# A three-stage kernel: second block's decays made in the pre-phase, silu issued ahead of the next weight tile's scaling, and block 1's units in steps 0, 1, 3 and 5

## The chip, the cores and the metric

The kernel runs on one core of a Trainium2 chip. The time is device time in microseconds (us) of one launch, as the median of several runs; lower is better. The engines are TensorE (PE, with its weight loads as PEld), VectorE (DVE), ScalarE (ACT), GpSimd (POOL) and the queues of SyncE (SP), each of which works through its own instructions in the order in which they were written.

## The reference

Three computations follow one another. The first is a chunked linear recurrence over 4 batches x 8 heads x 768 tokens (head 32, state 16):

```python
cum = np.cumsum(log(a)); L = np.exp(cum_i - cum_j) * causal      # per chunk of 32
y  = (C B^T * L) @ x + (C @ state) * np.exp(cum)
state = exp(sum) * state + sum_j B_j x_j exp(cum_end - cum_j)
```

The result, laid out as 3072 tokens x 256, goes through a gated layer, and that through a routed layer in which each token takes the one expert of eight with the largest logit:

```python
g = x @ w_gate; x = (g / (1 + exp(-g)) * (x @ w_val)) @ w_out     # 1536 hidden
h = np.maximum(x[mask] @ w1[e], 0); out[mask] = gate_w * (h @ w2[e])   # e = argmax
```

## The kernel before

Tokens are taken as 24 units of 128 tokens (six to a batch) and 6 blocks of 512 tokens (four units each). Block b is ready for the gated layer when its four units have written the tile `xt` of block b.

A unit u is made by these helpers: `weigh` (L268) multiplies x by a decay weight into `xw`, on DVE in the first blocks; `scores_mm` (L276) makes on PE the products of C and B and the sums for the state (both in `pc`); `scores_m` (L296) masks `pc` into `mt` on DVE; `states` (L303) carries the state with two DVE operations (`sv`, `se`) and two ACT copies (`st`); `values_mm` (L326) multiplies on PE into `py`; `values_out` (L352) multiplies by the decays `U` in four DVE operations (`y`, `z`) and casts to the high half of `xt` on ACT; `values_low` (L371) makes the low half on DVE. The decays of a whole block are made by `emit_d` (L247: four ACT operations into the tile `du` for blocks 1 and 2) and `emit_u` (L259: two PE matmuls into `pu`, two ACT copies into `U`).

The gated layer has 12 hidden tiles f of 128. Each number is held as a high and a low half, so each product is three matmuls. The weights arrive as 64-bit numbers (`load_w`) and are decoded for one hidden tile by `decode` (L391) in four parts: part 0 scales the high words into `ha` on ACT; part 1 puts the words together in three DVE operations into `wv`; part 2 casts the high half `wh` on ACT; part 3 makes the low half `wl` on DVE. A step for a block and a hidden tile is `mlp1_mm` (L420: six matmuls into `pg`, six into `pv`, in the order high, high, low of the weights for each half of the contraction), `mlp1_h` (L436: silu of `pg` on ACT into `h`, then times `pv` on DVE), `mlp1_split` (L442: `hh` on ACT, `hl` on DVE) and, two steps later (LAG = 2), `mlp1_down` (L449: six matmuls).

`first_block` writes all this out by hand for blocks 0 and 1. In a pre-phase it makes the four units of block 0, one after another, with matmuls that have no result (`keep_busy`) in PE's gaps. A loop of 24 steps follows: steps 0 to 5 are hidden tiles 0 to 5 of block 0, steps 6 to 11 the same for block 1, steps 12 to 23 the other six tiles of both. The table `units` says which step carries which unit (unit 4 to 7 are block 1, unit 8 and after block 2), the table `todo` which step decodes which hidden tile. Nothing reorders: the order of the code is the order of each engine's queue. PSUM is shared out as three buffers of tag "a" (`pc` and half of `py`, and `pu`), three of tag "g" (`pg`, `pv`, half of `py`), and two for the sums of `mlp1_down`; a matmul that takes a buffer waits until its last reader is done. The SBUF tag "mt" has two buffers, which `mt` and `du` share.

Of the kernel before, what the change touches and what calls it, by code (L numbers as in the profile page):

```python
# [9 lines left out]
F32 = mybir.dt.float32  # L10
# [18 lines left out]
BLK = 512  # L29
# [91 lines left out]
def kernel(  # L121
# [14 lines left out]
    def ps_a(shape, name):  # L136
        return ps.tile(shape, F32, tag="a", bufs=3, name=name)

    def ps_g(name, shape=(128, BLK)):
        return ps.tile(list(shape), F32, tag="g", bufs=3, name=name)  # L140
# [17 lines left out]
    u_t = {}  # L158
# [39 lines left out]
    def keep_busy(n):  # L198

        if not idle_t:  # L200
            idle_t.append(ps.tile([128, 2, 256], F32, tag="y0", bufs=1, name="pi"))
        for _ in range(n):
            nc.tensor.matmul(out=idle_t[0], lhsT=r32[:, 0],  # L203
                             rhs=r32.rearrange("p g j -> p (g j)").unsqueeze(1).to_broadcast([128, 2, 256]),
                             start=True, stop=True)
# [41 lines left out]
    def emit_d(b):  # L247
        d = ap_.tile([128, 4, 128], F32R, name="du", tag="mt", bufs=2)
        o = C_MU + 4 * (b % 2)
        if b in (1, 2):  # L250
            for q in range(4):
                nc.scalar.activation(out=d[:, q], in_=er[:, b // 2, 0:128], func=AF.Copy, scale=c1[:, o + q:o + q + 1])
        else:
            nc.gpsimd.tensor_tensor(
                out=d, in0=er[:, b // 2, 0:128].unsqueeze(1).to_broadcast([128, 4, 128]),
                in1=c1[:, o:o + 4].unsqueeze(2).to_broadcast([128, 4, 128]), op=ALU.mult)
        return d

    def emit_u(b, d=None):  # L259
        if d is None:  # L260
            d = emit_d(b)
        u_t[b] = ap_.tile([128, 4, 4, 64], F32, name="U", tag="U", bufs=1)
        for g in range(2):
            p = ps_a([128, BLK], "pu") if b else ps_g("pu")
            nc.tensor.matmul(out=p, lhsT=r32[:, g], rhs=d.rearrange("p a b -> p (a b)"), start=True, stop=True)
            nc.scalar.copy(out=u_t[b][:, :, 2 * g:2 * g + 2], in_=p.rearrange("p (o a i) -> p o a i", o=4, a=2))

    def weigh(u, e):  # L268

        r = raw[u]  # L270
        b, o = divmod(u, 4)
        r["xw"] = ap_.tile([128, 8, 32], F32, name="xw", tag="xw", bufs=3)
        e.tensor_tensor(out=r["xw"], in0=r["x"], in1=W[:, b, o * 8:o * 8 + 8].unsqueeze(2).to_broadcast([128, 8, 32]),
                        op=ALU.mult)
# [116 lines left out]
    def decode(f, *parts):  # L391


        if f >= NF:
            return
        for part in parts:
            lo, hi = wr[f][:, :, 0], wr[f][:, :, 1]
            if part == 0:
                ha_t[f] = mp.tile([128, 768], F32, name="ha", tag="ha", bufs=2)
                nc.scalar.activation(out=ha_t[f], in_=hi.bitcast(F32), func=AF.Copy, scale=2.0 ** -112)  # L400
            elif part == 1:
                v = wv_t[f] = mp.tile([128, 768], I32, name="wv", tag="wv", bufs=2)
                nc.vector.tensor_scalar(out=v, in0=lo, scalar1=29, scalar2=None, op0=ALU.logical_shift_right)
                nc.vector.scalar_tensor_tensor(out=v, in0=ha_t.pop(f).bitcast(I32), scalar=3, in1=v,
                                               op0=ALU.logical_shift_left, op1=ALU.bitwise_or)
                nc.vector.scalar_tensor_tensor(out=v, in0=hi, scalar=-0x80000000, in1=v,
                                               op0=ALU.bitwise_and, op1=ALU.bitwise_or)
            elif part == 2:
                nc.scalar.copy(out=wh[:, f], in_=wv_t[f].bitcast(F32))
            else:  # L410
                nc.vector.tensor_tensor(out=wl[:, f], in0=wv_t.pop(f).bitcast(F32), in1=wh[:, f].bitcast(F32),
                                        op=ALU.subtract)
# [7 lines left out]
    def mlp1_mm(b, c, m, f):  # L420

        xt = xt_t[b]
        cs = slice(c, c + m)
        p = []
        for i in range(2):
            t = ps_g("pg" if i == 0 else "pv")[:, 0:m]
            n = 0
            for k in range(2):
                o = i * 256 + k * 128
                for w, xp in ((wh, 0), (wh, 1), (wl, 0)):  # L430
                    nc.tensor.matmul(out=t, lhsT=w[:, f, o:o + 128], rhs=xt[:, xp, k, cs], start=n == 0, stop=n == 5)  # L431
                    n += 1
            p.append(t)
        return p
# [355 lines left out]
    def first_block():  # L790

        setup_loads()
        load(0)
        load_w(0)
        load(1)
        load(2)
        load_w(1)
        load(3)
        load_w(2)
        nc.sync.dma_start(out=c2, in_=I["cst"][:, C1:C_END])  # L800
        load_w(3)
        setup_ln()
        setup_ones()
        setup_decay()
        setup_cum(0, 1)
        keep_busy(2)
        weigh(0, nc.vector)
        scores_mm(0)
        cum_split(0, 1)
        scores_m(0)  # L810
        emit_u(0, emit_d(0))
        cum_store(0, 1, cum_ends(0, 1, cum_ends_d(0, 1)))
        states(0)
        cum_pairs(1, 8)
        keep_busy(3)
        decode(0, 0)
        for u in range(4):
            weigh(u + 1, nc.vector)
            scores_mm(u + 1)
            values_mm(u)  # L820
            if u == 1:
                setup_cum(1, 2)
            keep_busy((5, 7, 8, 10)[u])
            decode(u // 2, 3 if u % 2 else 1)
            scores_m(u + 1)
            if u % 2 == 0:
                decode(u // 2, 2)
            values_out(u)
            states(u + 1)
            values_low(u)  # L830
            if u % 2:
                decode(u // 2 + 1, 0)
            load(u + 4)
            if u == 1:
                silu_first()
        d = emit_d(1)
        load_w(4)

        todo = {0: 2, 1: 3, 2: 4, 3: 5, 6: 6, 8: 7, 10: 8, 12: 9, 14: 10, 15: 11}
        units = {0: 4, 1: 5, 3: 6, 4: 7, 13: 8, 16: 9, 19: 10, 22: 11}  # L840
        for i in range(2 * NF):
            q, f = divmod(i, HALF)
            b, f = q % 2, f + HALF * (q // 2)
            u = units.get(i)
            w = todo.get(i, NF)
            if i + 1 in units and units[i + 1] > 4:
                weigh(units[i + 1] + 1, nc.vector if i < 16 else nc.gpsimd)
            if i == 0:
                weigh(5, nc.vector)
            p = mlp1_mm(b, 0, BLK, f)  # L850
            if i == 0:
                emit_u(1, d)
            if u is not None:
                scores_mm(u + 1)
                values_mm(u)
            if len(late) == LAG:
                mlp1_down(*late.pop(0))
            late.append((b, 0, BLK, f))
            decode(w, 1)
            if w < NF:  # L860
                load_w(w + 3)
                decode(w + 1, 0)
            h = mlp1_h(p, BLK)
            decode(w, 2)
            if u is not None:
                values_out(u)
            decode(w, 3)
            if i >= 20:
                turn_y(0, i - 20)
            mlp1_split(h, b, 0, BLK, f)  # L870
            if i in (7, 13):
                take_part(0 if i == 7 else 1)
            if i == 19:
                take_y(0)
            if u is not None:
                values_low(u)
                if u != 7:
                    scores_m(u + 1)
                    states(u + 1)
                load(u + 4)  # L880
            if i == 6:
                scores_m(8)
                cum_split(1, 2)
            if i == 7:
                dd.append(cum_ends_d(1, 2))
            if i == 8:
                cum_store(1, 2, cum_ends(1, 2, dd.pop()))
                cum_pairs(8, NU)
                states(8)
            if i == 9:  # L890
                dd.append(emit_d(2))
            if i == 10:
                emit_u(2, dd.pop())
            if 16 <= i < 20:
                setup_route(i - 16)
            if i == 21:
                dd.append(emit_d(3))
            if i == 23:
                emit_u(3, dd.pop())
# [193 lines left out]
```

## Time and profile before

| | |
|---|---|
| median of 3 runs | 551.43 us (550.49 to 553.5) |
| the profiled execution's own time | 551.91 us |
| its span, first to last instruction | 550.1 us |
| mean granted TensorE clock | 0.981 |
| PE busy | 514.1 us (93%) |
| DVE busy | 298.1 us (54%) |
| ACT busy | 212.8 us (39%) |
| POOL busy | 98.6 us (18%) |

The profiled execution is 0.48 us longer than the median, and its span 1.8 us shorter than its own time. A share of busy time is an average over the whole span; the two blocks that the change touches lie in its first 67 us. Matmuls are pipelined, so that PE's busy time is not PE at its peak.

### The profile page before, as it was taken

Reading aid. Unit: us, or ns where it says so; the run is one execution under the profiler, and the core shown is the slowest. Engines: PE = TensorE matmul, PEld = TensorE weight load, DVE = VectorE, ACT = ScalarE, POOL = GpSimd, SP = SyncE. Lnnn points to the kernel's source line nnn. Section 1 sums busy time; section 2 is a strip of 40 time slices with the busy share of each in tenths; the row PEclk is TensorE's granted clock in tenths of the full one; section 3 lists DMA queues with packets and bytes.
Section 4 is the critical chain, followed back from the end, with each engine's and each line's share of the span. In section 5 each row is a group of like instructions: output and inputs, shape, how many; then the busy total and the mean of one; then the engine's idle time right before and its main releaser. Section 6 shows DMA issues by size and latency. Waiting matters only on the chain.

```text
span 550.1 us, 11255 instructions
## 1 busy us (share of the span) xinstructions
PE 514.1 (93%) x4599; PEld 423.9 (77%) x4599; DVE 298.1 (54%) x648; ACT 212.8 (39%) x394; POOL 98.6 (18%) x120
## 2 busy tenths in 40 slices
PE   5788799999998999999999999999997999999990
PEld 3566688778876777887778778888896999898980
DVE  4879787775453454445443554354374655646320
ACT  3554446533232333333333333434452443544320
POOL 0000000221003040002200034302027424250211
PEclk9899999999999899999999999999998999999995
DMA  8654332121020132103100102434056534431100
GB/s 317 251 174 155 135 108 84 40 50 39 21 98 2 20 98 41 39 20 98 21 1 2 41 2 86 147 116 39 2 192 78 184 94 150 149 113 47 38 11 31
DMA packets 20551, 45.85 MB, mean 83 GB/s; under 512 B 4624, under 2 KB 8080, under 8 KB 20496
## 3 DMA queue, kind: packets, MB, share of 16 engines
q1 hardware_dynamic: 17280, 38.39, 22.3%
q0 software_dynamic: 3072, 6.41, 4.6%
q8 instruction: 37, 0.61, 0.6%
q10 hardware_dynamic: 144, 0.30, 0.2%
q14 instruction: 18, 0.15, 0.1%
HBM read 38.59 MB, written 6.50 MB: 82 GB/s over the span
## 4 chain that ended last, share of the span: by engine, by line
PE 76%; issue 11%; DVE 4%; POOL 2%; ACT 2%; DMA 1%; another core or an unknown queue 1%; SPq 0%; POOLq 0%; ACTq 0%; DVEq 0%
PE py L459 18%; PE pg L431 18%; PE pv L431 17%; PE ph L741 6%; PE po L762 6%; PE pt L543 2%; PE pc L292 2%; POOL out L776 2%; PE pi L203 1%; PE py L348 1%; PE py L338 1%; PE pc L286 1%; PE px L730 1%; POOL xg L700 1%
## 5 line engine op out<-in xcount | busy, mean ns | idle before, releaser
L431 PE MATMUL pg<-xt,wh 128*128 128x512 f32 x288 | 93.7, 407 | 0.9 <-ACT h L438 0.9
L431 PE MATMUL pv<-xt,wh 128*128 128x512 f32 x288 | 90.8, 396 | 1.5 <-DVE h L439 1.5
L439 DVE TENSOR_TENSOR h<-h,pv 128x512 f32<-128x512 f32 x72 | 49.4, 687 | 69.1 <-PE pv L431 57.6
L446 DVE TENSOR_TENSOR hl<-h,hh 128x512 fp32r<-128x512 f32 x72 | 50.1, 695 | 64.1 <-ACT hh L445 61.7
L741 PE MATMUL ph<-xt,hl 128*128 128x512 f32 x288 | 74.0, 399 | 0.0
L762 PE MATMUL po<-hl,hh 128*128 128x256 f32 x384 | 71.3, 286 | 2.8 <-issue 2.8
L431 PEld LDWEIGHTS pv<-xt,wh 128*128 128x128 f32 x288 | 54.4, 189 | 14.7 <-DVE h L439 1.9
L762 PEld LDWEIGHTS po<-hl,hh 128*128 128x128 f32 x384 | 60.8, 190 | 5.2 <-issue 3.2
L431 PEld LDWEIGHTS pg<-xt,wh 128*128 128x128 f32 x288 | 52.6, 190 | 11.8 <-ACT h L438 1.5
L741 PEld LDWEIGHTS ph<-xt,hl 128*128 128x128 f32 x288 | 52.4, 191 | 9.7
L445 ACT CAST hh<-h 128x512 fp32r<-128x512 f32 x72 | 44.6, 620 | 38.8 <-DVE h L439 38.8
L459 PE MATMUL py<-hh,wh 128*128 128x512 f32 x144 | 58.7, 408 | 0.0
L438 ACT ACTIVATE h<-pg 128x512 f32<-128x512 f32 x72 | 42.8, 594 | 39.8 <-PE pg L431 39.6
L431 PE MATMUL pg<-xt,wl 128*128 128x512 f32 x144 | 57.3, 398 | 0.0
L459 PE MATMUL py<-hh,wl 128*128 128x512 f32 x144 | 56.8, 395 | 0.0
L459 PE MATMUL py<-hl,wh 128*128 128x512 f32 x144 | 56.8, 395 | 0.0
L431 PE MATMUL pv<-xt,wl 128*128 128x512 f32 x144 | 56.8, 394 | 0.0
L601 POOL DMA_INDIRECT slots<-ids,si x24 | 25.4, 1058 | 171.0 <-DVE si L593 166.2
L762 PE MATMUL po<-hl,hl 128*128 128x256 f32 x192 | 54.4, 283 | 0.4 <-issue 0.2
L750 DVE SCALAR_TENSOR_TENSOR hl<-ph,hh 128x512 fp32r<-128x512 f32 x48 | 33.1, 689 | 34.3 <-ACT hh L749 32.4
L749 ACT ACTIVATE hh<-ph 128x512 fp32r<-128x512 f32 x48 | 28.8, 600 | 42.0 <-PE ph L741 22.2
L762 PEld LDWEIGHTS po<-hl,hl 128*128 128x128 f32 x192 | 36.5, 190 | 0.9 <-issue 0.4
(140 smaller groups left out, 675.8 us busy)
## 6 DMA issues: line engine op xcount, KB each, us to landing
eraw<-in_ew SPq DMA_DIRECT2D x24, 512.0 KB
wraw<-in_mw SPq DMA_DIRECT2D x12, 768.0 KB
xbb<-in_xbb SPq DMA_DIRECT2D x24, 256.0 KB
cbd<-in_cbd SPq DMA_DIRECT2D x24, 256.0 KB
yd<-yr SPq DMA_DIRECT2D x6, 528.0 KB
slots<-ids,si POOLq DMA_INDIRECT x24
xg<-yd,idx POOLq DMA_INDIRECT x24
out<-ob,idx POOLq DMA_INDIRECT x24
```

The source lines that it names most:

```text
L292: nc.tensor.matmul(out=r["pc"][g][32 * q:32 * q + 32, 0:256], lhsT=r["bt"][k, 32 * q:32 * q + 32], rhs=r["c"][k, q // 2].rearrange("p h i ...
L431: nc.tensor.matmul(out=t, lhsT=w[:, f, o:o + 128], rhs=xt[:, xp, k, cs], start=n == 0, stop=n == 5)
L438: nc.scalar.activation(out=h, in_=p[0], func=AF.Silu)
L439: nc.vector.tensor_tensor(out=h, in0=h, in1=p[1], op=ALU.mult)
L445: nc.scalar.copy(out=hh, in_=h)
L446: e.tensor_tensor(out=hl, in0=h, in1=hh.bitcast(F32), op=ALU.subtract)
L459: nc.tensor.matmul(out=yb[b][d][:, c:c + m], lhsT=w[:, f, o:o + 128], rhs=h, start=first and n == 0, stop=last and n == 2, skip_group_chec ...
L601: i = nc.gpsimd.indirect_dma_start(out=slots[0:E * upto], out_offset=bass.IndirectOffsetOnAxis(ap=si[:, s:s + 1], axis=0), in_=ids[g][:, o ...
L741: nc.tensor.matmul(out=p, lhsT=self.hl[:, w, o:o + 128], rhs=self.xt[:, xp, k], start=n == 0, stop=n == 5)
L749: nc.scalar.activation(out=hh, in_=p, func=AF.Relu)
L750: nc.vector.scalar_tensor_tensor(out=hl, in0=p, scalar=0.0, in1=hh.bitcast(F32), op0=ALU.max, op1=ALU.subtract)
L762: nc.tensor.matmul(out=self.po[s // 2][:, s % 2], lhsT=h[:, q], rhs=self.hl[:, w, o:o + DM], start=f == 0 and n == 0 and s % 2 == 0, stop= ...
```

## The change

Four edits, all in the order in which `first_block` writes its work, and one in a buffer count:

- `emit_d(1)` moves from behind the pre-phase into its second unit (u = 1), and `emit_u(1)` from step 0 of the loop into the pre-phase's third unit (u = 2), where two of the eight matmuls without result are taken out. Its two `pu` tiles are now of tag "g". The tile `U` gets two buffers instead of one.
- In every step `mlp1_h` is written ahead of `load_w` and of part 0 of the next tile's decode.
- Unit 7 moves from step 4 to step 5, and stands there ahead of the step's `mlp1_mm` (its low half, `values_low`, too).
- The decode of hidden tile 5 moves from step 3 to step 4.

```diff
     def emit_u(b, d=None):
...
-        u_t[b] = ap_.tile([128, 4, 4, 64], F32, name="U", tag="U", bufs=1)
+        u_t[b] = ap_.tile([128, 4, 4, 64], F32, name="U", tag="U", bufs=2)
         for g in range(2):
-            p = ps_a([128, BLK], "pu") if b else ps_g("pu")
+            p = ps_a([128, BLK], "pu") if b > 1 else ps_g("pu")
...
             if u == 1:
                 setup_cum(1, 2)
-            keep_busy((5, 7, 8, 10)[u])
+            if u == 1:
+                d = emit_d(1)
+            if u == 2:
+                emit_u(1, d)
+            keep_busy((5, 7, 6, 10)[u])
...
-        d = emit_d(1)
         load_w(4)
 
-        todo = {0: 2, 1: 3, 2: 4, 3: 5, 6: 6, 8: 7, 10: 8, 12: 9, 14: 10, 15: 11}
-        units = {0: 4, 1: 5, 3: 6, 4: 7, 13: 8, 16: 9, 19: 10, 22: 11}
+        todo = {0: 2, 1: 3, 2: 4, 4: 5, 6: 6, 8: 7, 10: 8, 12: 9, 14: 10, 15: 11}
+        units = {0: 4, 1: 5, 3: 6, 5: 7, 13: 8, 16: 9, 19: 10, 22: 11}
...
+            if u == 7:
+                scores_mm(u + 1)
+                values_mm(u)
+                values_out(u)
+                values_low(u)
             p = mlp1_mm(b, 0, BLK, f)
-            if i == 0:
-                emit_u(1, d)
-            if u is not None:
+            if u is not None and u != 7:
                 scores_mm(u + 1)
                 values_mm(u)
...
             decode(w, 1)
+            h = mlp1_h(p, BLK)
             if w < NF:
                 load_w(w + 3)
                 decode(w + 1, 0)
-            h = mlp1_h(p, BLK)
             decode(w, 2)
-            if u is not None:
+            if u is not None and u != 7:
                 values_out(u)
...
             if u is not None:
-                values_low(u)
                 if u != 7:
+                    values_low(u)
                     scores_m(u + 1)
                     states(u + 1)
                 load(u + 4)
```

On ACT, this is what stands before in the pre-phase from the exponential `er` (made in unit 1, the input of `emit_d`) to the cast `wh` of hidden tile 1 in unit 2:

```order
L194 ACTIVATE er<-pe 128x264
L369 CAST xt<-y_329 128x2x128
L321 ACTIVATE st<-se,eb 128x64
L322 ACTIVATE st<-sv,eb 128x64
L400 ACTIVATE ha<-wraw 128x768
L210 ACT_TABLE_LOAD
L210 ACTIVATE sf<-c_69 128x1
L409 CAST wh<-wv 128x768
```

And this is what stands there now:

```order
L194 ACTIVATE er<-pe 128x264
L252 ACTIVATE du<-er,c_69 128x128 x4
L369 CAST xt<-y_334 128x2x128
L321 ACTIVATE st<-se,eb 128x64
L322 ACTIVATE st<-sv,eb 128x64
L400 ACTIVATE ha<-wraw 128x768
L210 ACT_TABLE_LOAD
L210 ACTIVATE sf<-c_69 128x1
L266 COPY U<-pu 128x4x128 x2
L409 CAST wh<-wv 128x768
```

The four `du` operations now stand ahead of unit 1's cast to `xt`, and the two copies to `U` ahead of the cast `wh`.

On ACT at the start of the loop, from the last operations of the pre-phase to the first cast of step 0, before:

```order
L322 ACTIVATE st<-sv,eb 128x64
L400 ACTIVATE ha<-wraw 128x768
L252 ACTIVATE du<-er,c_69 128x128 x4
L266 COPY U<-pu 128x4x128 x2
L400 ACTIVATE ha<-wraw 128x768
L438 ACTIVATE h<-pg 128x512
L409 CAST wh<-wv 128x768
```

And now:

```order
L322 ACTIVATE st<-sv,eb 128x64
L400 ACTIVATE ha<-wraw 128x768
L438 ACTIVATE h<-pg 128x512
L400 ACTIVATE ha<-wraw 128x768
L409 CAST wh<-wv 128x768
```

The first silu (`h`) has nothing of the decays ahead of it, and stands ahead of the scaling `ha` of hidden tile 3.

On DVE, from the low half `hl` of step 2 on, before (the `xw` is unit 8's, the three `wv` are hidden tile 5's, the `h` step 3's, `y` and `z` unit 6's):

```order
L446 TENSOR_TENSOR hl<-h,hh 128x512
L273 TENSOR_TENSOR xw<-xbb,W 128x256
L403 TENSOR_SCALAR wv<-wraw 128x768
L404 SCALAR_TENSOR_TENSOR wv<-ha,wv 128x768
L406 SCALAR_TENSOR_TENSOR wv<-wraw,wv 128x768
L439 TENSOR_TENSOR h<-h,pv 128x512
L364 TENSOR_TENSOR y_869<-py,U 128x192
L365 TENSOR_TENSOR z_870<-py,U 128x64
L366 TENSOR_TENSOR y_869<-py,U 128x64
L367 TENSOR_TENSOR y_869<-y_869,z_870 128x64
L411 TENSOR_TENSOR wl<-wv,wh 128x768
L446 TENSOR_TENSOR hl<-h,hh 128x512
```

Now `h` of step 3 and unit 6's first three operations on `py` follow the `hl` of step 2 at once; then come these (the first `hl` is step 3's, the `mt`, `sv` and `se` are unit 7's, the last `h` is step 4's):

```order
L367 TENSOR_TENSOR y_856<-y_856,z_857 128x64
L446 TENSOR_TENSOR hl<-h,hh 128x512
L375 TENSOR_TENSOR xt<-y_856,xt 128x2x128
L300 TENSOR_TENSOR mt<-pc,c_69 128x256 x2
L316 SCALAR_TENSOR_TENSOR sv<-se,eb,pc 128x64
L319 SCALAR_TENSOR_TENSOR se<-sv,eb,pc 128x64
L273 TENSOR_TENSOR xw<-xbb,W 128x256
L403 TENSOR_SCALAR wv<-wraw 128x768
L404 SCALAR_TENSOR_TENSOR wv<-ha,wv 128x768
L406 SCALAR_TENSOR_TENSOR wv<-wraw,wv 128x768
L439 TENSOR_TENSOR h<-h,pv 128x512
L411 TENSOR_TENSOR wl<-wv,wh 128x768
```

`xw` of unit 8 and the decode of hidden tile 5 now stand behind all of step 3's work and unit 7's state, and unit 7's own `y` follows only after this `wl`.

## Rows read from the trace of the kernel before

**Rows 1.** The page: busy us of the engines, and granted clock in 40 slices.
```profile
PE 514.1 (93%) x4599; PEld 423.9 (77%) x4599; DVE 298.1 (54%) x648; ACT 212.8 (39%) x394; POOL 98.6 (18%) x120
...
PEclk9899999999999899999999999999998999999995
```

**Rows 2.** Waits of PE, 0 to 64 us: who waited <- for whom, us, times, longest.
```profile
PE pc L286 <- DVE sv L316: 1.7, 1, 1.7
PE pv L431 <- DVE h L439: 1.5, 1, 1.5
```

**Rows 3.** Timeline, pre-phase: start us, us, engine, line, operation [idle before <- releaser].
```profile
19.67 0.39 ACT L194 ACTIVATE er<-pe 128x264 f32<-128x264 f32 x1 [3.69 <-PE pe L192]
19.96 0.40 ACT L369 CAST xt<-y 128x256 fp32r<-128x256 f32 x1
...
20.39 0.43 DVE L375 TENSOR_TENSOR xt<-y,xt 128x256 fp32r<-128x256 f32 x1 [0.46 <-ACT xt L369]
...
23.71 0.84 ACT L409 CAST wh<-wv 128x768 fp32r<-128x768 f32 x1 [0.55 <-DVE wv L406]
...
25.17 0.40 ACT L369 CAST xt<-y 128x256 fp32r<-128x256 f32 x1 [0.62 <-DVE y L367]
```

**Rows 4.** Timeline, loop step 0.
```profile
30.42 0.62 PE L431 MATMUL pg<-xt,wh 128*128 128x512 f32 x2
...
30.65 1.27 ACT L252 ACTIVATE du<-er,c 128x128 fp32r<-128x128 f32 x4
...
33.63 1.07 ACT L266 COPY U<-pu 128x512 f32<-128x512 f32 x2 [1.71 <-PE pu L265]
...
35.43 0.61 ACT L438 ACTIVATE h<-pg 128x512 f32<-128x512 f32 x1
...
36.68 0.35 DVE L364 TENSOR_TENSOR y<-py,U 128x192 f32<-128x192 f32 x1
```

**Rows 5.** Timeline, DVE and ACT in loop steps 2 to 4.
```profile
51.98 0.69 DVE L446 TENSOR_TENSOR hl<-h,hh 128x512 fp32r<-128x512 f32 x1
...
52.58 0.42 DVE L273 TENSOR_TENSOR xw<-xbb,W 128x256 f32<-128x256 f32 x1
...
54.49 0.96 DVE L406 SCALAR_TENSOR_TENSOR wv<-wraw,wv 128x768 int32<-128x768 int32 x1
...
55.37 0.68 DVE L439 TENSOR_TENSOR h<-h,pv 128x512 f32<-128x512 f32 x1
55.49 0.83 ACT L409 CAST wh<-wv 128x768 fp32r<-128x768 f32 x1 [2.59 <-DVE wv L406]
...
56.63 0.95 DVE L411 TENSOR_TENSOR wl<-wv,wh 128x768 fp32r<-128x768 f32 x1
...
57.71 0.69 DVE L446 TENSOR_TENSOR hl<-h,hh 128x512 fp32r<-128x512 f32 x1
...
59.62 0.28 DVE L319 SCALAR_TENSOR_TENSOR se<-sv,eb,pc 128x64 f32<-128x64 f32 x1
```

**Rows 6.** Timeline of PE: step 5, start of step 6, and unit 8.
```profile
62.53 0.62 PE L431 MATMUL pg<-xt,wh 128*128 128x512 f32 x2
...
66.71 0.64 PE L431 MATMUL pg<-xt,wh 128*128 128x512 f32 x2
...
99.42 0.34 PE L286 MATMUL pc<-xw,xbb 64*32 64x64 f32 x16
...
100.82 0.50 PE L459 MATMUL py<-hh,wh 128*128 128x512 f32 x1
```

**Rows 7.** The chain that ended last: start us, us, what.
```profile
13.96 2.44 issue
...
174.34 5.28 another core or an unknown queue
...
180.87 2.56 PE pg L431 x6
183.43 1.67 PE pv L431 x6
```

## The prediction

> **What bounds the kernel now.** I read the page first: PE is busy 514.1 us of 550.1, and its granted clock is down in three places only, near 16 us, near 180 us and at the end [rows 1]. So nearly all the time is matmuls that the change doesn't touch, and what it can win are the holes in PE. The waits of PE in the first 64 us came next. Two of them lie in the step of unit 7: 1.7 us until DVE has made `sv`, which frees the buffers for unit 8's products, and 1.5 us until DVE has multiplied `h` [rows 2]. Both times DVE is what is late. Then I read the timelines of the pre-phase and of steps 0 to 4 [rows 3 to 5]. In step 0 the silu `h` begins at 35.43, though PE began the step at 30.42 and needs half of it for `pg`: `du` and the copies to `U`, which wait for PE's `pu`, stand ahead of it on ACT [rows 4]. DVE can only then multiply `h` and go on to unit 4's `y` at 36.68. From there to the last `se` of unit 7 at 59.62 it has almost no idle time, and the steps run at its pace.
>
> From 62.53 PE no longer waits: step 5 takes from 62.53 to 66.71, 4.18 us for its 18 matmuls, or 0.232 us each [rows 6]. Whatever moves the start of step 6, now 66.71, moves the end of the kernel by as much.
>
> **The pre-phase, +1.2 us.** `emit_d(1)` puts four operations ahead of unit 1's cast to `xt`. They took 1.27 us together [rows 4], of which the last overlaps with what comes behind it; I take 1.2 us. Their input `er` is made at 19.67 and the cast followed at 19.96 [rows 3], so the cast now comes at about 21.15. DVE waited for that cast with the low half at 20.39 [rows 3], and behind the low half stands the `xw` of unit 3, on which PE's next products wait. So units 2 and 3 and the loop start later by the 1.2 us: 31.6 instead of 30.42. A second wait is new: `mt` of unit 2 must now wait until PE has read that of unit 1, since `du` has the other buffer. On PE that reading stands ahead of the matmuls for `er`, so it is over before 19.67; `y` follows `mt` within the time that ACT spends on `du`, and I cost it at nothing.
>
> The two copies to `U` (1.07 us [rows 4]) now stand between the silu table's first use and `wh` of tile 1. There ACT was idle for 0.55 us ahead of `wh` and for 0.62 us ahead of the next cast to `xt` [rows 3], 1.17 us together, so they are hidden, with 0.1 us to spare. If that cover fails they cost up to 1.07 us more, which gives 2.3 us as the upper end; the lower end is nothing, if the casts were not what unit 3 waits for. Two matmuls for `pu` take the place of two without result.
>
> **Step 0, -1.9 us.** The two `pu` matmuls go, and `h` has only `ha` of tile 2 ahead of it, which belongs to the pre-phase. PE makes 12 matmuls from 31.6 to 34.4 (2.8 us at 0.232). Unit 4's matmuls follow; an undisturbed unit takes 1.40 us, from 99.42 to 100.82 [rows 6], so `y` of unit 4 can begin on DVE at about 35.9 to 36.0. The silu is done by then, since `pg` is complete at about 33.2. Before, `y` began at 36.68, which is 6.26 us after the loop's start; now it is 4.4 us after it. With the pre-phase DVE is 0.7 us ahead of before.
>
> **Steps 0 to 2, nothing.** DVE has the same operations in the same order from this `y` to the `hl` of step 2, so the 0.7 us stay: that `hl` moves from 51.98 [rows 5] to 51.3. Silu ahead of `ha` buys nothing here, because DVE, not ACT, sets the pace; where ACT has room the order of two of its operations is free. From step 6 on PE doesn't wait in the trace, so there it buys nothing either.
>
> **Steps 3 to 5, -1.1 us.** Now I add up DVE's new row from intervals of the old one [rows 5]. From `hl` to the next operation are 0.6 us: `h` of step 3 at 51.9. From `h` to `hl` of the same step, with unit 6's `y`, its cast on ACT and `hh` between them, 2.34 us (55.37 to 57.71; the `wl` that stood there lay in the wait for `hh`): 54.25. From `hl` over the low half of `xt` and `mt` to `se` 1.91 us: 56.15. Then 0.3 us to `xw` of unit 8, and from `xw` to the last `wv` 1.91 us (52.58 to 54.49): 58.35. From there to `wh` on ACT 1.00 us, and `wh` itself takes 0.83: 60.2. `wl` takes 0.95 us: 61.15.
>
> PE meanwhile has steps 3 and 4 behind it without a wait (`pv` of step 4 needs `h` of step 3, done at 52.6) and stands at unit 8's products at about 56.4. It gets `xw` at 56.9, and is done with unit 7 at 58.3. Now the new wait: step 5 multiplies by hidden tile 5, whose decode was put one step later. PE waits 1.9 us for `wh` until 60.2, does two matmuls, and waits again for `wl` until 61.2. Of the 18 matmuls, ten of the first twelve and the six of `mlp1_down` are left after that, 16 x 0.232 = 3.7 us. Step 6 begins at 64.9 instead of 66.71. So of the 3.2 us of waits that go [rows 2] a good part comes back, as 2.4 us of other waits. The tail of unit 7 isn't late: behind `wl` come `hl`, `y`, a cast and the low half of `xt`, about 2.3 us, done by 63.5.
>
> **The sum.** 1.2 - 1.9 - 1.1 = -1.8 us, so the profiled execution's 551.91 would be 550.1. That execution is 0.48 us over the median; against the median of 551.43 the forecast is 549.6. The second `U` buffer changes nothing that PE waits for later.
>
> **Rivals.** *The clock falls.* The new wait of PE in step 5 is 1.9 us and, two matmuls later, 0.5 us, after another 0.5 us shortly before. In the trace the clock went to half (1.2 of 2.4 GHz) after PE had stood idle for 2.44 us from 13.96 on, and again after the stall at 174.34 [rows 7]; after the single waits of 1.5 and 1.7 us [rows 2] it did not. What stands against it is that the new idle time is broken by two matmuls. The price: after 180.87 six `pg` matmuls took 2.56 us and six `pv` 1.67 us [rows 7] instead of 1.40 each, so 1.4 us more; with what was hit ahead of them I take 1.7. Then the gain is gone: 551.3.
>
> The Trainium skill, TensorE: Matmul & The Clock Gate, Part 1, says that half rate is the default which activity lifts, and that what the gate watches runs freely, not from the kernel's start, so that the point of a change moves between runs. By that rule it is a matter of where the new wait falls, and the time is either 549.6 or 551.3; the trace, in which 2.44 us of idle time were enough, doesn't contradict it.
>
> *PE sets the pace of step 5.* If DVE's row were 2.9 us shorter than I add it up, step 5 would begin at 58.3 and the gain would be 4.7 us: 546.7. For it speaks that DVE's share is only 54% [rows 1]; against it, that every interval in the row was measured under the same load.
>
> *DVE's row is longer: slower.* Four operations in the new row wait for ACT within steps 3 to 5 (`hl`, `wl`, `hl`, the low half of `xt`), and I allowed in full for the first two alone. Step 6 needs the low half of unit 7, which I have at 63.5. Each wait can cost about one cast and its turn, up to 1.2 us. The kernel is slower once unit 7 or `wl` is 1.8 to 3.2 us later than I have it; with four such waits in full, 4.8 us on the last of them, step 6 begins at 68.3, 1.6 us later than before: 553.0. Against it: all of these queues had the same neighbours before.
>
> *The stall at 174.34.* DVE stood 5.28 us there for something the profile doesn't name [rows 7]. The order of instructions there isn't changed. Should another layout make it go, the time would be about 545.
>
> **How the numbers follow.** The forecast gets 0.50, the fallen clock 0.27, PE's pace 0.09, the longer row 0.09, the stall 0.05. The forecast's own range is 548.4 to 550.7, from the bounds of the pre-phase (0 to 2.3 us instead of 1.2). The range that takes in the fallen clock and most of the other cases is 547.0 to 552.3. About 0.5% (2.8 us) is what a measurement of this kernel can tell from no change, so faster means under 548.7 and slower over 554.2. Faster is PE's pace, the stall and a tail of the forecast: 0.24. Slower is a tail of the longer row: 0.04. The rest, 0.72, is no change that can be told.
>
> **What would show it.** In the changed kernel's profile, unit 1's cast to `xt` should begin near 21.2, step 0 near 31.6, `y` of unit 4 near 36.0, and `wl` of tile 5 should end near 61.2 with PE waiting for it and for `wh`; step 6 should begin near 64.9. A step 5 without a wait, a clock at 0.5 between 58 and 66 us, or `U` copies ahead of a late `wh` in the pre-phase would each prove one step wrong.

## The result and the profile after

The changed kernel takes 547.35 us (median of 13 runs, 544.38 to 552.03), the kernel before 551.43 us beside it (13 runs, 547.15 to 554.1). The ratio is 0.9917, with an interval of 0.989 to 0.9943: 0.8% faster, where the forecast was 549.6 us and no change that can be told. The profiled execution went from 551.91 to 547.26 us, its span from 550.1 to 545.5 us.

The page of the changed kernel, the two lines that answer to [rows 1]:

```profile
PE 512.3 (94%) x4597; PEld 422.2 (77%) x4597; DVE 297.8 (55%) x648; ACT 212.7 (39%) x394; POOL 97.5 (18%) x120
...
PEclk9899899999999999999999999999998999999996
```

In the clock row, slice 5 (54.5 to 68 us) has become an 8, and slice 14 (near 180 us), an 8 before, is a 9. Both kernels have a further 8 near 420 us, which the prediction's count of three places left out. So the clock fell at a new place and no longer falls at an old one. The waits of PE up to 66 us (who waited <- for whom: us, times, longest) show what [rows 2] became:

```profile
...
PE pg L431 <- ACT wh L409: 1.8, 1, 1.8
PE py L338 <- DVE h L439: 0.7, 1, 0.7
PE pc L286 <- DVE xw L273: 0.5, 1, 0.5
PE pc L286 <- DVE mt L300: 0.4, 1, 0.4
...
```

The waits for `sv` and for `h` are gone, and the forecast wait of step 5 for `wh` is there with 1.8 us. Next the timeline of the pre-phase and of step 0 (start us, us, engine, line, operation), as [rows 3, 4] before:

```profile
19.79 0.39 ACT L194 ACTIVATE er<-pe 128x264 f32<-128x264 f32 x1 [3.73 <-PE pe L192]
20.08 1.27 ACT L252 ACTIVATE du<-er,c 128x128 fp32r<-128x128 f32 x4
21.25 0.39 ACT L369 CAST xt<-y 128x256 fp32r<-128x256 f32 x1
...
24.46 1.07 ACT L266 COPY U<-pu 128x512 f32<-128x512 f32 x2
25.42 0.85 ACT L409 CAST wh<-wv 128x768 fp32r<-128x768 f32 x1
26.45 0.40 ACT L369 CAST xt<-y 128x256 fp32r<-128x256 f32 x1 [0.19 <-DVE y L367]
...
31.55 0.62 PE L431 MATMUL pg<-xt,wh 128*128 128x512 f32 x2
33.14 0.60 ACT L438 ACTIVATE h<-pg 128x512 f32<-128x512 f32 x1 [1.26 <-PE pg L431]
35.92 0.36 DVE L364 TENSOR_TENSOR y<-py,U 128x192 f32<-128x192 f32 x1 [0.62 <-PE py L348]
```

The loop begins 1.13 us later and unit 4's `y` 0.76 us earlier. (Where step 0 begins differs by up to 1 us between profiles of kernels with the same pre-phase; see below the table.) Then the end of DVE's row and step 5, as [rows 5, 6] before:

```profile
51.23 0.69 DVE L446 TENSOR_TENSOR hl<-h,hh 128x512 fp32r<-128x512 f32 x1
...
56.08 0.28 DVE L319 SCALAR_TENSOR_TENSOR se<-sv,eb,pc 128x64 f32<-128x64 f32 x1
...
59.21 0.83 ACT L409 CAST wh<-wv 128x768 fp32r<-128x768 f32 x1 [1.35 <-DVE wv L406]
60.08 0.96 DVE L411 TENSOR_TENSOR wl<-wv,wh 128x768 fp32r<-128x768 f32 x1 [0.30 <-ACT wh L409]
60.10 0.95 PE L431 MATMUL pg<-xt,wh 128*128 128x512 f32 x2 [1.84 <-ACT wh L409]
61.09 0.80 PE L431 MATMUL pg<-xt,wl 128*128 128x512 f32 x1
...
66.17 0.63 PE L431 MATMUL pg<-xt,wh 128*128 128x512 f32 x2
```

`wl` ends at 61.04, and step 6 begins at 66.17, only 0.54 us earlier than before. Why it isn't earlier is in two stretches of PE (us, busy us and instructions of PE, PEld, DVE, ACT and POOL, granted clock, DMA):

```profile
60.44:63.86 3.42, 3.38 (x9) 2.19 (x8) 2.42 (x7) 1.13 (x3) 0.00 (x0) 0.50 0.83 327
66.20:69.60 3.40, 3.40 (x16) 2.79 (x15) 3.12 (x5) 1.58 (x4) 0.00 (x0) 1.00 0.00 0
```

Nine matmuls ran in 3.42 us at the granted clock of 0.50, where 16 run at 1.00: the clock was at its lower level, 1.2 of 2.4 GHz.

The rest of the gain came where the change had moved nothing. From step 6 to step 28 both kernels keep the same pace, the changed one 0.54 us ahead (step 28 starts at 170.49 and 169.95). Step 29 begins 3.40 us earlier, step 30 4.96 us, and from step 31 on it is about 4.5 us to the end. (Steps 24 to 35 are the hidden tiles of block 2, so step 28 is its fifth, which carries unit 13.) In step 28 PE makes the products `py` of unit 13, and DVE's `y` waits for them. First the rows of the kernel before:

```profile
174.74 0.52 PE L348 MATMUL py<-cbd,st 64*32 64x64 f32 x28
...
179.60 0.36 DVE L364 TENSOR_TENSOR y<-py,U 128x192 f32<-128x192 f32 x1 [5.26 <-remote]
...
180.01 0.85 PE L543 MATMUL pt<-iw,yT 128*128 128x136 f32 x4 [3.17 <-DVE y L364]
```

And the same rows after the change:

```profile
174.18 0.52 PE L348 MATMUL py<-cbd,st 64*32 64x64 f32 x28
...
176.22 0.36 DVE L364 TENSOR_TENSOR y<-py,U 128x192 f32<-128x192 f32 x1 [2.43 <-PE py L348]
...
176.63 0.73 PE L543 MATMUL pt<-iw,yT 128*128 128x136 f32 x4 [0.33 <-issue]
```

In both PE has written `py` long before `y` starts: 4.3 us before, 1.5 us after. That is the 5.28 us row of the chain in [rows 7]. PE stood still for 3.2 us in one and 0.3 us in the other, and only in the kernel before did the clock go to half behind it.

### The profile page after: what moved, and what is told of

The parts are those of the page before. It is cut to its first block, busy times and chain, and to the rows that moved or that the text cites. A ratio compares the mean times of both kernels' runs of the same rounds, so it can differ in the third digit from the quotient of the medians.

```text
span 545.5 us, 11245 instructions
## 1 busy us (share of the span) xinstructions
PE 512.3 (94%) x4597; PEld 422.2 (77%) x4597; DVE 297.8 (55%) x648; ACT 212.7 (39%) x394; POOL 97.5 (18%) x120
## 4 chain that ended last, share of the span: by engine, by line
PE 76%; issue 11%; DVE 5%; POOL 2%; ACT 2%; DMA 1%; another core or an unknown queue 0%; SPq 0%; POOLq 0%; ACTq 0%
PE py L459 18%; PE pg L431 18%; PE pv L431 17%; PE ph L741 7%; PE po L762 6%; PE pt L543 2%; PE pc L292 2%; POOL out L776 2%; PE py L348 1%; PE py L338 1%; PE pi L203 1%; PE pc L286 1%; PE px L730 1%; DVE hl L446 1%; DMA at<-in_at 1%
## 5 line engine op out<-in xcount | busy, mean ns | idle before, releaser
L762 PEld LDWEIGHTS po<-hl,hh 128*128 128x128 f32 x384 | 60.5, 190 | 5.8 <-ACT hh L749 3.8
L601 POOL DMA_INDIRECT slots<-ids,si x24 | 25.4, 1058 | 167.1 <-DVE si L593 162.3
```

Source lines behind the costliest of these rows:

```text
L601: i = nc.gpsimd.indirect_dma_start(out=slots[0:E * upto], out_offset=bass.IndirectOffsetOnAxis(ap=si[:, s:s + 1], axis=0), in_=ids[g][:, o ...
L762: nc.tensor.matmul(out=self.po[s // 2][:, s % 2], lhsT=h[:, q], rhs=self.hl[:, w, o:o + DM], start=f == 0 and n == 0 and s % 2 == 0, stop= ...
```

## The experiments

For each kernel I read the start of loop step 0, the time from there to step 6, and the length of step 28, all as starts of the step's first `pg` matmul in the timeline. Ratios are to the kernel before run on the same chip, with their intervals. "Scatters" are block 0's four indirect DMAs of POOL (`route_c(0, ...)`, L601), which stand in steps 27 to 30 and which POOL issues between 168.7 and 173.2 us in the kernel before.

| kernel | step 0 at | 0 to 6 | step 28 | median us | ratio |
|---|---|---|---|---|---|
| before | 30.42 | 36.29 | 10.02 | 551.43 | |
| changed | 31.55 | 34.62 | 7.16 | 547.35 | 0.9917 (0.989 to 0.9943) |
| decays only | 31.67 | 34.40 | 11.34 | 551.05 | 0.9976 (0.9949 to 1.0004) |
| units only | 30.57 | 35.24 | 10.52 | 552.19 | 0.9989 (0.9958 to 1.0021) |
| before, scatters later | 29.59 | 36.30 | 6.25 | 546.32 | 0.99 (0.9864 to 0.9936) |
| changed, scatters later | 30.63 | 34.65 | 6.27 | 545.33 | 0.9883 (0.984 to 0.9925) |
| changed, again | 31.75 | 34.54 | 7.46 | 543.74 | 0.9914 (0.9897 to 0.993) |
| before, fillers in four | 38.19 | 36.34 | 6.25 | 548.98 | 0.9982 (0.9956 to 1.0009) |
| decode put back, scatters later | 30.87 | 33.40 | 6.25 | 539.32 | 0.9842 (0.9824 to 0.9859) |
| the same, decays a unit later | 29.45 | 33.39 | 6.25 | 538.72 | 0.9822 (0.9808 to 0.9837) |
| that, scatters in place | 30.49 | 33.41 | 11.59 | 544.51 | 0.9901 (0.9872 to 0.993) |
| before, silu order, scatters later | 29.89 | 35.47 | 6.25 | 540.82 | 0.9859 (0.9843 to 0.9876) |
| before, small fillers | 30.99 | 36.29 | 6.25 | 543.64 | 0.9913 (0.9896 to 0.993) |
| before, again (one run) | 30.14 | 36.31 | 11.22 | 547.74 | |

The runs were made on several chips, and two things move its numbers that have nothing to do with the kernels' differences.

First, medians from different chips can't be compared. In six profiles (the first pair, decays only, units only, and the two kernels with nothing but the scatters later) PE waits once for 2.1 to 5.0 us between 411 and 422 us, and the clock goes to half there. From the start of the last loop step to the end these six take 167.5 to 170.5 us; the other eight, on two other chips, have no such wait and take 163.1 to 163.3. For the kernel before itself it is 168.2 us in its first profile and 163.1 in its second, so this doesn't belong to the kernel. The row of the first profile (waits of PE behind 64 us):

```profile
PE po L762 <- issue: 3.0, 2, 2.8
```

The changed kernel had the like in its first profile (168.0 us), so the first pair can be compared.

Second, the start of step 0 moves without an edit: 30.42, 30.57 and 29.59 in three kernels whose pre-phase is the same. In the pre-phase PE waits 2.44 us in each of them, and the clock fell at that wait in the first two and not in the third. These are the wait in the kernel before with the scatters later, and its clock row, whose second slice is a 9 where [rows 1] has an 8:

```profile
16.43 0.32 PE L286 MATMUL pc<-xw,xbb 64*32 64x64 f32 x13 [2.44 <-issue]
...
PEclk9999999999999999999999999999997999999995
```

So of the columns, "0 to 6" is the steady one: 36.29 to 36.34 us in all five profiles of kernels that leave steps 0 to 5 as they were.

### Parts of the change alone

Only the first edit, the decays:

```diff
-        u_t[b] = ap_.tile([128, 4, 4, 64], F32, name="U", tag="U", bufs=1)
+        u_t[b] = ap_.tile([128, 4, 4, 64], F32, name="U", tag="U", bufs=2)
...
+            if u == 1:
+                d = emit_d(1)
+            if u == 2:
+                emit_u(1, d)
+            keep_busy((5, 7, 6, 10)[u])
...
```

> Only the first edit: the second block's decays made in the pre-phase, U with two buffers; silu order, units and decodes as before. Theory A (the working of the forecast): loop step 0 starts 1.2 us later, unit 4's y on DVE 0.7 us earlier, and that 0.7 us stays to step 6: -0.7 us, a ratio of 0.9987; whatever the time shows beyond that comes from the stall near 174 us, where PE lost about 5 us in the profile of before and about 1 us in that of the changed kernel. Theory B (the edits are worth the whole 4 us in the first 67 us): about -1.5 us or more, and step 6 starts at 65.2 or earlier.

Measured: the loop starts 1.25 us later, steps 0 to 5 take 1.9 us less, step 6 begins 0.6 us earlier. These are the forecast's two terms. But step 28 took 11.34 us, so no gain can be told in the time. The longest wait of PE behind 66 us in this kernel:

```profile
PE pt L543 <- DVE y L364: 4.0, 1, 4.0
```

Only the tables and unit 7's new place:

```diff
-        todo = {0: 2, 1: 3, 2: 4, 3: 5, ...
-        units = {0: 4, 1: 5, 3: 6, 4: 7, ...
+        todo = {0: 2, 1: 3, 2: 4, 4: 5, ...
+        units = {0: 4, 1: 5, 3: 6, 5: 7, ...
...
+            if u == 7:
+                scores_mm(u + 1)
+                values_mm(u)
+                values_out(u)
+                values_low(u)
...
```

> Only the units and the decode moved (unit 7 to step 5 ahead of its products, tile 5's decode to step 4); decays and silu order as before. Theory A: step 6 starts 1.1 us earlier than before if the clock holds through step 5, and 0.3 us later if it falls to half there as it did in the profile of the changed kernel: ratio 0.998 to 1.0005. Theory B: step 6 starts 2.5 us or more earlier, ratio 0.9955.

Measured: steps 0 to 5 take 1.05 us less, near the forecast's term for steps 3 to 5 (-1.1). Step 5 of this kernel has the same two waits, and its clock stays at 1.00 behind them:

```profile
60.99 0.73 PE L431 MATMUL pg<-xt,wh 128*128 128x512 f32 x2 [1.81 <-ACT wh L409]
61.98 0.50 PE L431 MATMUL pg<-xt,wl 128*128 128x512 f32 x1 [0.26 <-DVE wl L411]
```

So each of these two alone is worth about what the forecast said, and neither has the gain at step 28 that the whole change has. The third edit, the order of the silu, wasn't run alone with the scatters in place, and no run has these two without it; so which combination brings that gain is open. The third edit isn't enough by itself: a later version has it and loses 5.3 us in step 28.

### The scatters a round later

One line, in the kernel before and in the changed kernel:

```diff
-            if b == 2 and 3 <= f < 7:
+            if b == 3 and 3 <= f < 7:
                 route_c(0, f - 3)
```

> The kernel before with the first four scatters of slots (those of block 0, which POOL issues in block 2's steps 3 to 6) put into the same steps of block 3. Theory A (the stall near 174 us belongs to the first scatters): the stall leaves step 28 of the loop, and the time falls by 3 to 5 us (ratio 0.991 to 0.995), unless it comes back at the scatters that are now the first, near 198 us. Theory B (it belongs to the place in the code, or to chance): the stall stays near 174 us, ratio 1.000.

> The changed kernel with the same move of the first four scatters. Theory A: the stall costs the changed kernel only about 1 us, so the time falls by 0 to 1 us against the changed kernel, and the difference to the kernel before with the same move is only what the first 67 us give, 0.5 to 1.8 us. Theory B: the difference between the two stays about 4 us.

Measured: step 28 takes 6.25 and 6.27 us. This is `y` in the kernel before with the scatters later; it follows `py` at once:

```profile
174.11 0.36 DVE L364 TENSOR_TENSOR y<-py,U 128x192 f32<-128x192 f32 x1 [0.62 <-PE py L348]
```

That one line is worth 1% (0.99), as much as the whole change; by the traces steps 28 to 30 take 5.3 us less, and step 0 begins 0.8 us earlier, since the clock didn't fall ahead of it. The loss doesn't come back at the scatters of block 1, which are now the first: from step 31 to the last step it takes 191.0 us, and 190.9 before. With the loss out of both, the ratios differ by 0.17%, 0.9 us, which is within their intervals; in the traces step 6 begins at 65.28 instead of 65.89.

### The change a second time

The same kernel, for a second profile.

> The changed kernel once more, for a second profile. Theory A (the pause at the first scatters is met in every execution, and its length for PE varies): the same 0.992 of before, step 6 near 66 us with the clock at half from about 60 us on, and near 174 us DVE held up between h of step 28 and the end of unit 9's y by about 5 us, of which PE loses 1 to 4. Theory B (the change removes the pause's cost for good, by where its instructions stand): PE loses about 1 us there again.

Measured: 0.9914, the same gain. The clock fell at 60.5 us again, and step 28 took 7.46 us. Steps 28 to 30 together, which take 15.17 us where nothing is lost, took 16.54 us in the first profile and 18.01 here. So the loss of the changed kernel is small in both, but it isn't fixed: 1.4 and 2.8 us, against 5.3 in the kernel before and 6.5 in that kernel's second profile (below).

### PE's instructions shifted, scatters in place

The filling matmuls of the pre-phase, each split in four of 128 columns:

```diff
-        for _ in range(n):
-            nc.tensor.matmul(out=idle_t[0], lhsT=r32[:, 0],
-                             rhs=r32.rearrange("p g j -> p (g j)").unsqueeze(1).to_broadcast([128, 2, 256]),
+        for _ in range(4 * n):
+            nc.tensor.matmul(out=idle_t[0][:, 0, 0:128], lhsT=r32[:, 0], rhs=r32[:, 0], start=True, stop=True)
```

> The kernel before, with each of the 35 matmuls without result in the pre-phase split into four of a quarter of the columns: 105 more matmuls in about the same time, so that PE's later instruction fetches fall 105 of its matmuls earlier. Theory C (the pause comes of PE's instruction fetch meeting the first scatters on the DMA engines: in before the fetch began at 7.6 us after the start of step 28, and with the scatters moved at 4.8 us): the fetch falls ahead of step 28, the pause goes, and the time falls by 4 to 5 us, ratio 0.991. Theory D (the scatters alone hold up PE's semaphores): the pause stays near 174 us, ratio 1.000.

A miss in its price: the loop began 7.8 us late. These are two rows of it:

```profile
15.63 4.53 PE L203 MATMUL pi<-r 128*128 128x128 f32 x20
...
28.55 3.79 PE L203 MATMUL pi<-r 128*128 128x128 f32 x32
```

The first twenty follow one another in 0.213 us, the later ones in 0.112 us, and the step between the two lies at 24.6 us; the trace has its first record of a granted clock, the full one, at 24.66 us in this kernel and at 9.82 in the kernel before. So the first ones ran at the lower clock, and even at the full one a quarter of the columns takes half of the time of a large one (0.232 us), not a quarter.

But step 28 took 6.25 us, though the scatters stood where they were. (The twelve runs of this kernel form two groups, near 545.1 and 549.2 us, and the profile is one of the second, so the ratio says little here.) Because the pre-phase had changed so much, I did it again with a filling that takes no more time:

```diff
-            keep_busy((5, 7, 8, 10)[u])
+            keep_busy((5, 7, 2, 10)[u])
+            if u == 2:
+                for j in range(30):
+                    nc.tensor.matmul(out=idle_t[0][0:32, 0, 0:64], lhsT=c1[0:64, C_R16:C_R16 + 32],
+                                     rhs=c1[0:64, C_MK:C_MK + 64], start=True, stop=True, tile_position=(0, 0))
```

> The kernel before with six of the eight filling matmuls of unit 2's pre-phase replaced by thirty small ones (32 x 64, on 64 rows), at about the same time. PE's instruction count up to loop step 28 is 24 matmuls larger, so PE fetches its instructions at other moments, and the scatters stay where they were. If the loss near 174 us comes about because a fetch of PE falls behind the scatters: step 28 takes 6.25 us or little more instead of 10.02, and the time is 4 to 5 us under before (546.5 to 547.5). If the semaphore updates alone are held back, wherever the fetch is: step 28 stays between 9 and 11 us and the time is that of before within 1 us. The start of the loop can move by up to 1 us by the filling.

Measured: 4.9 us faster than before (0.9913), with the loop starting 0.57 us later and steps 0 to 5 as long as before; step 47 took 6.14 us instead of 4.65, so 1.5 us are lost again there. The rows of step 28 in this kernel:

```profile
174.95 0.52 PE L348 MATMUL py<-cbd,st 64*32 64x64 f32 x28
...
175.50 0.36 DVE L364 TENSOR_TENSOR y<-py,U 128x192 f32<-128x192 f32 x1 [0.62 <-PE py L348]
...
176.91 0.62 PE L543 MATMUL pt<-iw,yT 128*128 128x136 f32 x4
```

`y` follows `py` within 0.03 us of its end by the rows, with the scatters under way as before: POOL issues them at the same distances from the start of step 28, to 0.02 us, in all nine profiles that have them there. So it isn't a matter of when the scatters come to PE's step 28. Neither the scatters nor anything in step 28 was touched. What changed is how many instructions PE has behind it when it gets there, and what the pre-phase does.

And the kernel before itself, for a second profile:

> The kernel before once more, for a second profile. If the loss near 174 us belongs to the kernel, loop step 28 takes between 9.5 and 11 us again and step 6 begins at 66.7 within 0.2. If it comes and goes from run to run, step 28 lies elsewhere between 6.25 and 12 us.

Measured: step 28 took 11.22 us, a little over what I gave, and step 6 began at 66.45, a little earlier than I gave. `y` in this second profile of the kernel before:

```profile
180.53 0.36 DVE L364 TENSOR_TENSOR y<-py,U 128x192 f32<-128x192 f32 x1 [6.49 <-remote]
```

The loss belongs to the kernel before, and varies by about 1 us.

### Versions that go further

The decode of tile 5 put back to step 3, where unit 6 still is, with the scatters later:

```diff
-        todo = {0: 2, 1: 3, 2: 4, 4: 5, ...
+        todo = {0: 2, 1: 3, 2: 4, 3: 5, ...
```

> The changed kernel with the first four scatters in block 3, and the decode of hidden tile 5 put back from step 4 to step 3 (unit 7 stays in step 5). By the DVE row: step 4 waits about 1.4 us for h of step 3, step 5 about 1.4 us for xw of unit 8, none of the waits for wh and wl of tile 5 is left, and the clock holds. Step 6 then begins 5 steps' worth later at 64.9 on the changed kernel's scale instead of 66.2: 1.3 us less than the changed kernel with the scatters moved, whose ratio was 0.9883. If the clock's fall cost nothing, the two are equal.

Measured: no wait for `wh`, no fall of the clock, and step 6 at 64.27. The wait that took its place in PE's list is DVE's `h`, 1.2 us at the longest:

```profile
PE pv L431 <- DVE h L439: 1.4, 2, 1.2
```

Steps 0 to 5 take 1.25 us less than in the changed kernel with the scatters later (33.40 and 34.65). The medians differ by far more, but these two kernels ran on different chips, and their ratios' intervals overlap. Then also the decays one unit later (`emit_d(1)` at the end of unit 2, `emit_u(1)` in unit 3, fillers 5, 7, 8, 8):

> As the run with the decode put back, and emit_d(1) moved on to the end of the pre-phase's third unit, emit_u(1) to its fourth, in place of two matmuls without result there. By the forecast's term for the pre-phase the four operations on ACT then lie in ACT's idle time of 3 us ahead of unit 3's cast and no longer delay unit 1's: step 0 begins at 30.5 to 30.8 instead of 31.6, and 0.9 us come off the run with the decode put back: about 2.2 us less than the changed kernel with the scatters moved.

Measured: 538.72 us, 0.9822 of before, the lowest of all, though its interval overlaps that of the run before it. Step 0 begins at 29.45, 1.42 us earlier than in that run, where 0.9 was expected; the 30.5 to 30.8 of the text counted from a profile in which the clock had fallen in the pre-phase, and here it didn't. The same kernel with the scatters left in place:

> The change with unit 6's decode put back to step 3, block 1's decays one unit later in the pre-phase and the scatters left where they were (loop steps 27 to 30). It shows what the scatters cost in a third layout. My theory (the loss near 174 us comes from PE's instruction fetch and semaphore updates being late behind the four scatters, and each layout meets it at its own place): loop step 28 is longer than 6.25 us again, by between 1 and 5 us, and the time is by as much over the 538.7 of the same kernel with the scatters a block step later, so 540 to 544. Rival (the loss belongs to the layout of before alone): step 28 takes 6.25 us and the time is 538.7 within 0.7.

Measured: step 28 takes 11.59 us, and by the ratios 0.8%, about 4.3 us, of the gain is gone. The profiled run is the slowest of six, 545.86 us, and lost 7.1 us in steps 28 to 30; the fastest took 540.46, 5.4 us less, so it can hardly have lost as much there. In this layout, then, the loss seems to differ from run to run; the other five have no profile. Its `y`:

```profile
177.91 0.36 DVE L364 TENSOR_TENSOR y<-py,U 128x192 f32<-128x192 f32 x1 [6.42 <-remote]
```

This kernel and the changed one have the same number of matmuls and differ only in the first 60 us, and yet one loses 5.3 us in step 28 and the other 0.9 (7.16 against 6.25).

### The order of the silu

The third edit alone, on the kernel before with the scatters later:

```diff
+            h = mlp1_h(p, BLK)
             if w < NF:
                 load_w(w + 3)
                 decode(w + 1, 0)
-            h = mlp1_h(p, BLK)
```

> Only the third edit of the change, the silu h ahead of the next tile's scaled words, on the kernel before with the scatters moved to loop steps of the next round, so that the loss near 174 us is out of the comparison. My theory (DVE sets the pace of steps 0 to 4, ACT has room): the same as that kernel without the edit, 546.3 within 1, and step 6 begins within 0.3 us of 65.9. Rival (the order of the two is worth what the whole change won more than I forecast): 2 us or more faster, with step 6 near 64.

A miss: steps 0 to 5 took 35.47 us instead of 36.30, 0.83 less. These are its rows on ACT in step 0:

```profile
33.10 1.07 ACT L266 COPY U<-pu 128x512 f32<-128x512 f32 x2 [1.71 <-PE pu L265]
34.06 0.62 ACT L438 ACTIVATE h<-pg 128x512 f32<-128x512 f32 x1
34.55 0.94 ACT L400 ACTIVATE ha<-wraw 128x768 f32<-128x768 f32 x1
```

With the decays still in step 0, ACT is what is late there, and `h` comes 4.2 us after the step's start instead of 5.0 (34.63 in the kernel with the other order). The two medians come from different chips, and their ratios' intervals overlap, so the 0.83 us of the timeline are what I take from it.

## Why the prediction was wrong, step by step

**Pre-phase, +1.2.** Right for this pair: 1.13 us, though the start of step 0 moves by up to 1 us between profiles. The cast came at 21.25 (forecast 21.15), step 0 at 31.55 (31.6). The copies to `U` were hidden, with little to spare as forecast: `wh` of tile 1 came 0.5 us later than its neighbours' shift, and the next cast still waited 0.19 us for DVE.

**Step 0, -1.9.** Right: unit 4's `y` at 35.92 (35.9 to 36.0).

**Steps 0 to 2, nothing.** Right for the row: `hl` at 51.23 (51.3). What the text said of the silu, that its order buys nothing, holds only with the decays gone from step 0, as the silu's own run showed; both edits take away the same delay of ACT.

**Steps 3 to 5, -1.1.** DVE's row came out as added up: `se` 56.08 (56.15), `wh` done at 60.04 (60.2), `wl` at 61.04 (61.15), PE's wait 1.84 (1.9). The end was not as forecast: from 61.09 the 16 matmuls took 5.08 us instead of 3.7, because the clock fell. This is the rival that had 0.27; its price was 1.7 and was 1.4 here. So steps 0 to 5 of the forecast were right but for this, and the first 67 us gave 0.54 us (0.16 between the second profiles of both kernels), where the forecast had 1.8 and the rival about nothing. The fall came in the same two matmuls in all three profiles of this layout (60.44, 60.46, and 59.58 where the loop began 0.9 us earlier), and not in the one profile of the kernel with the units alone, which has the same two waits. At the wait of about 2.44 us in the pre-phase it came in eight profiles and not in four. The rule of the Trainium skill (TensorE: Matmul & The Clock Gate, Part 1) that the point of a change moves between runs is neither borne out nor refuted by this: the four are all kernels with the scatters later, and the eight have them in place, though each of the four has its pre-phase in common with one of the eight. So the 2.44 us which the prediction called enough are not always enough, and what tells a wait that lowers the clock from one that doesn't isn't settled.

**The stall at 174.34: the step that failed.** I wrote that the order of instructions there isn't changed, and took the time as unchanged but for a chance of 0.05. It gave 3.9 of the 4.5 us that the profile won. So it was also wrong that whatever moves the start of step 6 moves the end by as much: step 6 moved by 0.54 us, the end of the span by 4.6. Two things are shown. The loss needs the scatters: moved a round later, it is gone in both kernels. And it needs more than the scatters: with other fillers 150 us earlier it is gone from step 28 too, in one profile each of two kernels, with the scatters in place. It goes with the layout for the most part: over steps 28 to 30 four layouts lost 5.3 to 7.1 us in their five profiles, the changed one 1.4 and 2.8 in its two. But it doesn't look as if it were of the layout alone: the runs of the last of the four spread over 5.4 us. So an edit in the first 40 us (the small fillers) can move 5 us at 175 us without touching anything there. That PE's place in its instruction stream is what counts is the likeliest reading and not shown: the two kernels with other fillers differ in their pre-phase as well, and the two with an equal number of matmuls lost 7.1 and 1.4 us. Why the change has less of the loss therefore stays open.

What the trace says of the mechanism is less than that. In the kernels with the loss PE's matmuls ran on time, but their semaphore updates, on which `y` and a load of SP wait, were recorded 4.6 to 6.1 us late. The packet in which PE's instructions seem to be fetched (a DMA queue of kind "instruction", 16 KB each, 37 packets for 4599 matmuls and 38 in the two kernels with more matmuls, so one for about 125 with their weight loads) came at 6.9 to 7.6 us of step 28, and at 4.8 us where the scatters were out of the way. In the kernel with small fillers it came at 4.8 us and the updates were on time, with the scatters in place. That fits a fetch that falls behind the scatters and holds up the updates; but the changed kernel has its fetch at 7.6 as well and loses little, since the one update that `y` needs came already at 6.25 us and the other at 8.9. Why its first update got through is open. And the kernel with the fillers in four has a packet at 7.0 us with the scatters in place: there it falls behind step 28, the next updates come 1.4 to 2.2 us late, and PE loses nothing.

Of the other rivals, PE's pace and the longer row didn't happen: DVE's row was right to 0.16 us throughout. (The price of PE's pace was added up wrongly: a step 5 that begins at 58.3 and takes 4.18 us ends at 62.5, a gain of 4.2 us and not 4.7.) The time lies inside the range given, but on the side that had a chance of 0.24: two rivals came true together, each with its sign, and I had added them up only one at a time.

## What to carry to other kernels

An engine's row added up from intervals of the old trace came out within a few tenths of a us here, so a short stretch can be forecast; what it wins must then be seen to reach the end. A wait in the chain that the profile gives to no engine ("another core or an unknown queue") isn't fixed because its code is: give it its whole length as a spread in every forecast, and move what runs beside it, since here one line at that place was worth as much as the four edits. When an edit puts a producer later to make room, look for the new wait of PE and price the clock behind it, not only the wait.

## What the runs showed of the hardware

- Where four indirect DMAs of POOL were issued 1.3 to 1.8 us apart, PE's semaphore updates came up to 6 us late while PE itself ran on (in the kernel before `py` was written at 175.26 and `y` begun at 179.60); with the DMAs elsewhere they were on time. In two of nine profiles with the DMAs in place the update for `y` was on time too.
- A matmul of 128 columns of these 32-bit numbers, with its weight load, took 0.112 us at the full clock (2.4 GHz) and 0.213 us before it was granted, and one of 512 columns 0.232 us at the full clock: a quarter of the columns cost half of the time.
- PE's clock fell to 1.2 GHz in step 5 after a wait of 1.84 us; before, a wait of 1.7 us [rows 2] had left it alone, and with the units alone one of 1.81 us did. At a wait of about 2.44 us in the pre-phase it fell in eight profiles and not in four.
